# A two-stage network behind a decaying linear attention: early loads in a tile that is used later, a transfer rate in the planner's table, and a range check that is planned with the rest

## Chip, cores, metric

One core of a Trainium2 chip. The metric is the time of the program on the device in microseconds (us), the median of several runs; less is better. PE is TensorE, DVE VectorE, ACT ScalarE, POOL GpSimd, and SP SyncE, which here does nothing but issue DMAs.

## The reference

All is float32. An attention with a complex decay runs along the sequence (4 batches, 8 heads, 768 steps, 48 columns a head); its output is 3072 tokens of 384 numbers. A softplus layer pair follows, then a gated one. Cut to what matters:

```python
scale = np.minimum(mag, 0.999) / (mag + 1e-06)      # mag = |a_re + i a_im|
for t in range(S):
    S_re, S_im = ar * S_re - ai * S_im + kv, ar * S_im + ai * S_re   # kv = k_t v_t^T
    y[:, :, t] = q_t @ S_re
x = y as (3072, 384)
h = x @ w_in                                        # 384 -> 2048
x = (max(h, 0) + log1p(exp(-|h|))) @ w_out          # 2048 -> 384
h = (x @ w1) * (x @ w2) @ w3                        # 384 -> 1024 -> 1024
out = h @ w_out2                                    # 1024 -> 384
```

The weights of the layers come as 64-bit floats, which the kernel turns into 32-bit ones by integer operations on DVE.

## The kernel before

**Attention.** The sequence is cut into 24 chunks `u` of 128 steps; `u = 4 j + b` for step group `j` and batch `b`. For each chunk `load` brings the decay `a` (128 x 768), `load_qk` queries and keys `qk` (128 x 768), `load_v` the values. `norm` (steps s1 to s4) computes the magnitude and the limited decay: ACT squares `a` into `nt`, DVE adds, ACT takes logarithm and exponential, DVE multiplies the result with `a` into a tile `PT`, which holds two chunks. The multiply `PT<-a,nt` is the last reader of `a`. `scan` forms running products over two chunks on DVE (`tm`, `PT`, `ET`: first within groups of 8 steps, then over the group ends, then back down). `inv` forms the scaled queries and keys `qkp` from `PT` and `qk`, stores them to DRAM (`pd`) and reads them back in another layout (`rs`). `mm` makes the scores `sc` on PE, masks them on DVE (`am`), and multiplies with the values and the state (`yp`, `stp`) into `y`.

**Softplus stage.** 3072 tokens in blocks: 128, 128, 256 tokens (blocks 0 to 2), then five of 512 (blocks 3 to 7). For each of 16 slices `f` of the hidden layer, `s1` multiplies (`s`), ACT forms exp(-|h|) and its logarithm, DVE adds (`g`), and `s2a` accumulates in `acc`. Blocks 0 to 2 use plain float32 (`s<-x,w`). From block 3 on each factor is split into a high and a low half (`ww..h`, `ww..l`; `xh`, `xl`; both halves of `g` in the tile `gg`) and three products take the place of one (`s<-xh`); the low halves of the weights are formed on DVE during block 2. The attention's chunks for the next block run beside the block before. In the last block the weights of the gated stage are converted (`w3t`, `w12t`, `wo2t`), and w3 and w_out2 are multiplied into one matrix (`wpa`).

**Gated stage.** For six blocks of 512 tokens `s3` computes `pa` and `pb`, DVE multiplies them (`bg`), `s2b` accumulates with the combined matrix. Beside it all raw weights are loaded once more and their range is checked on DVE (`ck`, `lims`). At the end four comparisons (`okp`, line 1091), a reduce (`ok`, 1094), a transpose on PE (`okt`, 1098) and a reduce to one number (`oki`, 1099) decide whether a general version has to run.

**What sets the order.** Nothing is issued as it is written. Up to line 1078 the code records every instruction into a `Plan` (`add`), with what it depends on and a cost from a table (`cost`, from line 124). `flush` then runs a list scheduling 16 times with changing priorities, keeps the plan that ends earliest by the table, and issues the instructions in that order, from one helper line, 196. Each engine then runs its own queue strictly in that order; all DMAs stand in SP's queue, and one that has to wait holds up those behind it. In the table a DMA from DRAM to the chip takes SP `size / 360` ns, at least 475, and is there 2500 + `size / 360` ns after its start.

**Room.** A tile with a tag and `bufs=n` waits until the n-th last tile of that tag has had its last reader. `a` has one buffer (chunk 1 takes tag `n2` instead), `qk` has one (`QB = 1`), `v` one. The tile `gg` of tag `GG` (6 x 512 numbers in each partition) is first written in block 3:

```python
s["a"] = ap.tile([P, 2, GT], F32, tag="n2" if u == 1 else "a", bufs=1, name=f"a{u}")
s["qk"] = ap.tile([P, 2, GT], F32, tag="qk", bufs=QB, name=f"qk{u}")
gg.append(ap.tile([P, 2, HB, NB], F32R, tag="GG", name="gg"))
```

Of the kernel before, what the change touches and what calls it, by code (L numbers as in the profile page):

```python
# [11 lines left out]
F32 = mybir.dt.float32  # L12
F32R = mybir.dt.float32r
I32 = mybir.dt.int32
AF = mybir.ActivationFunctionType
ALU = mybir.AluOpType
PSUM = bass.MemoryType.PSUM
DRAM = bass.MemoryType.DRAM

P = 128  # L20
B, H, SEQ, D = 4, 8, 768, 48
DM = H * D
NT = B * SEQ
T = 128
NCH = NT // T
CPB = SEQ // T
G = DM // P
GT = G * T
# [3 lines left out]
NB = B * T  # L32
# [15 lines left out]
S1B = 5  # L48
ATAG = "s1"
VB = 1  # L50
TML = 384
NTB = 1
QB = 1
# [19 lines left out]
class Plan:  # L73
# [50 lines left out]
    def cost(self, eng, op, outs, ins):  # L124
        n = max(self.free_size(x) for x in (*outs, *ins))
        if eng == "SP":
            size = 4
            for _, n in outs[0].ap:
                size *= n
            cost = max(650 if n < 512 and self.on_chip(ins[0]) else 475, size / 360)  # L130
            if not self.on_chip(outs[0]):
                land = 5200
            elif self.on_chip(ins[0]):
                land = 2300
            elif hasattr(ins[0].tensor, "tag_meta"):
                land = 6800
            else:
                land = 2500 + size / 360
            return cost, max(land - cost, 0)
        if eng == "PE":  # L140
            n = self.free_size(outs[0])
            if op == "transpose":
                return 109, 250
            m = outs[0].ap[0][1]
            if ins[0].dtype == F32R:
                return n / 2.4 + 14, 250
            return (0.75 * n + 24 if m <= 64 else max(n, m) / 0.6 + 5), 250
        if eng == "DVE":
            far = [x for x in ins if x.ap[-1][0] >= 4 and x.ap[-1][1] > 1]
            return 72 + n / (1.92 if op == "tensor_scalar" else 0.52 if len(far) > 1 else 0.95), 200  # L150
        if eng == "ACT":
            return 105 + 0.88 * n, 200
        return 160 + n * 2.08, 200

    def push(self, eng, call, pre, cost, lat):
        self.ops.append((eng, call, pre, cost, lat))
        return len(self.ops) - 1

    def add(self, engine, op, args, kw):
# [35 lines left out]
        def call():  # L195
            getattr(engine.unit, op)(*args, **kw)  # L196

        cost, lat = self.cost(engine.name, op, outs, ins)
        if self.group is None:
            me = self.push(engine.name, [call], pre, cost, lat)  # L200
# [155 lines left out]
def fused(ctx: ExitStack, tc: tile.TileContext, a_in, qk_in, v_in, wio, w12, w3t, wo2, q, k, v, a_re, a_im, outT):  # L356
    nc = tc.nc
    plan = Plan(tc)
    V, A, PE, GP, SP = plan.V, plan.A, plan.PE, plan.GP, plan.SP

    fast = ExitStack()
# [5 lines left out]
    cp = ctx.enter_context(tc.tile_pool(name="cp", bufs=1))  # L367
# [3 lines left out]
    ap = fast.enter_context(tc.tile_pool(name="ap", bufs=1))  # L371
# [3 lines left out]
    ident = cp.tile([P, P], F32, name="ident")  # L375
# [8 lines left out]
        out=trow[:, 0:1], in0=trow[:, 2:3], scalar1=W - 1, scalar2=L.bit_length() - 1,  # L384
# [3 lines left out]
        out=trow[:, 1:2], in0=trow[:, 3:4], scalar1=W.bit_length() - 1, scalar2=None, op0=ALU.logical_shift_right  # L388
# [7 lines left out]
    m2max = cp.tile([P, NCH], F32, name="m2max")  # L396
    pend = cp.tile([P, B, G], F32, name="pend")
    NCK = 2 * FA + 6 * FB
    wlim = cp.tile([P, 2], F32, name="wlim")
    ncheck = [0]  # L400

# [14 lines left out]
    def pst(tag, bufs, shape, name):  # L416
        return ps.tile(shape, F32, tag=tag, bufs=bufs, name=name)

    def att_ps(shape, name):
        return pst(ATAG, ATT, shape, name)  # L420

    def load(u):
        s = c[u]
        s["a"] = ap.tile([P, 2, GT], F32, tag="n2" if u == 1 else "a", bufs=1, name=f"a{u}")
        SP.dma_start(s["a"], a_in[u])

    def load_qk(u):
        s = c[u]
        s["qk"] = ap.tile([P, 2, GT], F32, tag="qk", bufs=QB, name=f"qk{u}")
        SP.dma_start(s["qk"], qk_in[u])  # L430

    def load_v(u):
# [274 lines left out]
    def feed(u):  # L707
        load_qk(u)
        load_v(u)
# [3 lines left out]
    def norms(us):  # L713
        out = []
        for u in us:
            out += norm(u)
            if u + 1 < NCH:
                out.append(lambda u=u: load(u + 1))
        return out
# [165 lines left out]
    def evac_out(s):  # L885
        for i in range(KC):
# [7 lines left out]
            )  # L894

    load(0)
    for f in range(4):
        w_load(f)
# [82 lines left out]
    for bi in range(nblk):  # L981
        last = bi == nblk - 1
        t0, n = BLOCKS[bi]
# [29 lines left out]
    def b_x(bi):  # L1013
        r = ap.tile([P, 2 * H * T], F32, tag="rs1", name=f"xr{bi}")[:, 0 : KC * NB]
        r = r.rearrange("p (k n) -> p k n", k=KC)
        SP.dma_start(r, x2d[bi])
        if bi % 2:
            h, l = (ap.tile([P, KC, NB], F32R, tag="P", bufs=2, name=f"bx{n}{bi}") for n in "hl")
        else:
            h, l = x_tiles((f"bxh{bi}", f"bxl{bi}"))  # L1020
        split(h, l, r)
        xb[bi] = (h, l)
# [30 lines left out]
    for i, n in enumerate(("min", "max")):  # L1053
        bst[n] = lims[:, i * NCK : (i + 1) * NCK]
    b_x(0)
    it = 0
    nit = (NBB - 1) * FB
    for bi in range(NBB):
        gq = {}
        for f in range(FB):  # L1060
# [5 lines left out]
            it += 1  # L1066
            while ncheck[0] < min(NCK, NCK * it // nit):
                src, n = cks[ncheck[0]]
# [5 lines left out]
    for i, n in enumerate(("min", "max")):  # L1074
        V.tensor_reduce(
            out=wlim[:, i : i + 1], in_=bst[n], axis=mybir.AxisListType.X, op=getattr(ALU, n)
        )
    plan.flush()
    V, PE = nc.vector, nc.tensor
    fast.close()  # L1080
    ep = ctx.enter_context(tc.tile_pool(name="ep", bufs=1))
    okp = ep.tile([P, B * G + NCH + 2], F32, name="okp")
    c0 = 0
    for src, lim, op in (
        (pend.rearrange("p b g -> p (b g)"), 1e-3, ALU.is_ge),
# [4 lines left out]
        n = src.shape[1]  # L1090
        V.tensor_scalar(out=okp[:, c0 : c0 + n], in0=src, scalar1=lim, scalar2=None, op0=op)
        c0 += n
    ok1 = ep.tile([P, 1], F32, name="ok1")
    V.tensor_reduce(out=ok1, in_=okp, axis=mybir.AxisListType.X, op=ALU.min)
    oki = ep.tile([1, 1], I32, name="oki")
    with tc.tile_pool(name="fps", bufs=1, space=PSUM) as fps:
        okt = fps.tile([1, P], F32, name="okt")
        PE.transpose(okt, ok1, ident)
        V.tensor_reduce(out=oki, in_=okt, axis=mybir.AxisListType.X, op=ALU.min)
    ok = nc.values_load(oki[0:1, 0:1], min_val=0, max_val=1)  # L1100
    with tc.If(ok < 1):
        general(tc, q, k, v, a_re, a_im, wio, w12, w3t, wo2, xg, outT)
# [211 lines left out]
```

## Time and profile before

| what | value |
|---|---|
| median of 3 runs | 992.73 us (989.97 to 993.53) |
| profiled execution, own time | 990.76 us |
| its span | 989.0 us |
| mean granted clock of PE | 0.981 |
| PE matmul, busy | 883.0 us (89%), 5353 instructions |
| DVE, busy | 766.9 us (78%), 1713 instructions |
| ACT, busy | 520.5 us (53%), 1025 instructions |
| HBM read and written | 108.00 MB and 28.31 MB |

How to read it: the span is the time from the first to the last instruction of one execution; the profiled execution's own time has 1.8 us around it. Busy shares are averages over stages with different bounds, so the rows further down go stage by stage. All planned instructions bear line 196; a group is known by its tile. A timeline row gives start, duration, engine, line, operation, output and inputs, and in brackets the idle time just ahead of it with what ended it.

### The profile page before, as it was taken

What the parts mean: (1) busy time and instruction counts of PE and PEld (TensorE: products, weight loads), DVE (VectorE), ACT (ScalarE), POOL (GpSimd) and SP (SyncE); (2) the same over time, 40 slices, a digit from 0 to 9 for tenths busy, and PEclk for the clock granted to TensorE, in tenths of its full rate; (3) what the DMA queues carried; (4) which work ended last, traced back from release to release, by engine and by line L of the source; (5) the groups of instructions that cost most, each with busy time, mean ns of one, the idle gap of its engine ahead of it and who ended that gap; (6) DMA issues with size and microseconds to landing.
All of it is one profiled execution on the core that took longest, in us unless ns stands there. A gap on an engine that the chain in (4) does not pass through costs nothing.

```text
span 989.0 us, 15040 instructions
## 1 busy us (share of the span) xinstructions
PE 883.0 (89%) x5353; PEld 750.2 (76%) x5353; DVE 766.9 (78%) x1713; ACT 520.5 (53%) x1025; POOL 6.0 (1%) x19
## 2 busy tenths in 40 slices
PE   0048698886999999999999999999999999999996
PEld 0038597775888888888888888888888877788885
DVE  8998789889969998998997866977878787422221
ACT  4238677555867885778686664754231222131221
POOL 2000000000000000000000000000000000000000
PEclk9997899998999999999999999999999999999999
DMA  8490536473681656456375752444787867110101
GB/s 316 181 274 13 151 93 160 99 166 100 130 189 34 163 136 138 130 124 157 69 199 110 210 167 78 141 126 125 233 275 234 269 203 250 57 32 1 32 1 36
DMA packets 89938, 138.56 MB, mean 140 GB/s; under 512 B 7936, under 2 KB 60544, under 8 KB 89856
## 3 DMA queue, kind: packets, MB, share of 16 engines
q1 hardware_dynamic: 89856, 137.53, 50.4%
q8 instruction: 44, 0.72, 0.3%
q14 instruction: 38, 0.31, 0.1%
HBM read 108.00 MB, written 28.31 MB: 138 GB/s over the span
## 4 chain that ended last, share of the span: by engine, by line
PE 71%; DVE 15%; DMA 8%; issue 3%; ACT 3%; SPq 0%; POOL 0%; DVEq 0%; ACTq 0%; POOLq 0%
PE acc L196 26%; PE s L196 18%; PE pa L196 8%; PE pb L196 8%; DMA a<-a_in 4%; PE wpa L196 3%; DVE tm L196 3%; DVE PT L196 3%; PE sc L196 3%; PE yp L196 3%; DMA ckr<-w3t 2%; DVE w L196 2%; DVE qkp L196 1%; PE stp L196 1%; ACT nt L196 1%
## 5 line engine op out<-in xcount | busy, mean ns | idle before, releaser
L196 ACT ACTIVATE g<-g 128x512 f32<-128x512 f32 (+2 forms) x256 | 130.1, 521 | 3.3
L196 ACT ACTIVATE g<-s 128x512 f32<-128x512 f32 (+2 forms) x128 | 62.2, 487 | 68.2 <-PE s L196 45.1
L196 DVE TENSOR_TENSOR bg<-pa,bg 128x512 f32<-128x512 f32 x48 | 32.8, 687 | 80.9 <-PE pa L196 80.8
L196 DVE SCALAR_TENSOR_TENSOR g<-s,g 128x512 f32<-128x512 f32 (+2 forms) x128 | 70.8, 556 | 22.8 <-ACT g L196 22.4
L196 ACT CAST gg<-bg 128x512 fp32r<-128x512 f32 x48 | 29.8, 621 | 99.7 <-DVE bg L196 99.7
L196 ACT COPY bg<-pb 128x512 f32<-128x512 f32 x48 | 28.1, 587 | 90.5 <-PE pb L196 78.4
L196 PE MATMUL s<-x,w 128*128 128x128 f32 (+1 forms) x288 | 55.2, 340 | 16.5 <-DVE g L196 8.3
L196 PE MATMUL ktp<-ident,qkp 128*128 128x128 f32 x120 | 20.3, 290 | 54.7 <-DVE qkp L196 52.1
L196 PE MATMUL sc<-rs 112*128 112x128 f32 x384 | 53.3, 289 | 12.5 <-DMA rs<-pd 10.2
L196 PEld LDWEIGHTS sc<-rs 112*128 112x128 f32 x384 | 51.4, 203 | 16.4 <-issue 10.8
L196 DVE CUSTOM_DVE_ANT_0 ck<-ckr 128x384 f32<-128x384 f32 x80 | 43.5, 543 | 24.9 <-DMA ckr<-w3t 10.3
L196 PEld LDWEIGHTS s<-x,w 128*128 128x128 f32 x288 | 46.5, 215 | 20.8 <-DVE g L196 8.7
L196 ACT CAST gg<-g 128x512 fp32r<-128x512 f32 x80 | 49.2, 615 | 21.3 <-DVE g L196 12.7
L196 DVE TENSOR_TENSOR PT<-tm 128x96 f32<-128x96 f32 x192 | 59.3, 345 | 0.9
L196 PEld LDWEIGHTS ktp<-ident,qkp 128*128 128x128 f32 x120 | 15.3, 148 | 58.7 <-issue 47.3
L196 DVE TENSOR_TENSOR gg<-g,gg 128x512 fp32r<-128x512 f32 x80 | 55.1, 690 | 4.9 <-ACT gg L196 4.0
L196 PE MATMUL acc<-g,w 128*128 128x128 f32 (+1 forms) x288 | 51.5, 319 | 1.9 <-DVE g L196 1.9
L196 PE MATMUL acc<-gg,bwp2h 128*128 128x512 f32 x144 | 49.4, 392 | 1.2 <-ACT gg L196 1.2
L196 PE MATMUL acc<-gg,bwp0h 128*128 128x512 f32 x144 | 49.0, 392 | 1.1 <-ACT gg L196 1.1
L196 DVE TENSOR_TENSOR tm<-PT 128x384 f32<-128x384 f32 x84 | 46.9, 558 | 0.8
L196 PEld LDWEIGHTS acc<-g,w 128*128 128x128 f32 x288 | 42.9, 199 | 4.5 <-DVE g L196 2.3
L196 DVE TENSOR_REDUCE lims<-ck 128x1 f32<-128x384 f32 x80 | 43.1, 538 | 2.3
(314 smaller groups left out, 2313.0 us busy)
## 6 DMA issues: line engine op xcount, KB each, us to landing
pd<-qkp SPq DMA_DIRECT2D x24, 768.0 KB, 4.7
rs<-pd SPq DMA_DIRECT2D x48, 384.0 KB, 6.4
wr<-wio SPq DMA_DIRECT2D x32, 384.0 KB, 7.3
ckr<-wio SPq DMA_DIRECT2D x32, 384.0 KB, 3.7
a<-a_in SPq DMA_DIRECT2D x24, 384.0 KB, 3.4
qk<-qk_in SPq DMA_DIRECT2D x24, 384.0 KB, 3.8
w3r<-w3t SPq DMA_DIRECT2D x16, 384.0 KB, 3.6
w12r<-w SPq DMA_DIRECT2D x16, 384.0 KB, 3.2
```

Source lines behind the costliest of these rows:

```text
L196: getattr(engine.unit, op)(*args, **kw)
```

## The change

1. In the table, `size / 360` becomes `size / 270` in both places.
2. A tile `early` of tag `GG`, 4 x 768 numbers in each partition, takes `a2`, `a3`, `qk1` and `qk2`. They no longer use the tags `a` and `qk`.
3. The range check's last part is recorded ahead of `plan.flush()`, so that the plan orders it: `okp` takes a tile of tag `v`, `okt` one of tag `s1`, and `oki` lives in the pool `cp`, which stays open.

```diff
@@ cost
-            cost = max(650 if n < 512 and self.on_chip(ins[0]) else 475, size / 360)
+            cost = max(650 if n < 512 and self.on_chip(ins[0]) else 475, size / 270)
...
-                land = 2500 + size / 360
+                land = 2500 + size / 270
@@ fused
+    oki = cp.tile([1, 1], I32, name="oki")
...
+    ahead = []
+
+    def early():
+
+        if not ahead:
+            ahead.append(ap.tile([P, 4, 2, GT], F32, tag="GG", name="early"))
+        return ahead[0]
+
     def load(u):
         s = c[u]
-        s["a"] = ap.tile([P, 2, GT], F32, tag="n2" if u == 1 else "a", bufs=1, name=f"a{u}")
+        if u in (2, 3):
+            s["a"] = early()[:, u - 2]
+        else:
+            s["a"] = ap.tile([P, 2, GT], F32, tag="n2" if u == 1 else "a", bufs=1, name=f"a{u}")
         SP.dma_start(s["a"], a_in[u])
 
     def load_qk(u):
         s = c[u]
-        s["qk"] = ap.tile([P, 2, GT], F32, tag="qk", bufs=QB, name=f"qk{u}")
+        if u in (1, 2):
+            s["qk"] = early()[:, u + 1]
+        else:
+            s["qk"] = ap.tile([P, 2, GT], F32, tag="qk", bufs=QB, name=f"qk{u}")
         SP.dma_start(s["qk"], qk_in[u])
...
-    plan.flush()
-    V, PE = nc.vector, nc.tensor
-    fast.close()
-    ep = ctx.enter_context(tc.tile_pool(name="ep", bufs=1))
-    okp = ep.tile([P, B * G + NCH + 2], F32, name="okp")
+    okp = ap.tile([P, DM], F32, tag="v", bufs=VB, name="okp")
...
-    ok1 = ep.tile([P, 1], F32, name="ok1")
-    V.tensor_reduce(out=ok1, in_=okp, axis=mybir.AxisListType.X, op=ALU.min)
-    oki = ep.tile([1, 1], I32, name="oki")
-    with tc.tile_pool(name="fps", bufs=1, space=PSUM) as fps:
-        okt = fps.tile([1, P], F32, name="okt")
-        PE.transpose(okt, ok1, ident)
-        V.tensor_reduce(out=oki, in_=okt, axis=mybir.AxisListType.X, op=ALU.min)
+    ok1 = okp[:, DM - 1 : DM]
+    V.tensor_reduce(out=ok1, in_=okp[:, 0:c0], axis=mybir.AxisListType.X, op=ALU.min)
+    okt = pst("s1", S1B, [P, NB], "okt")[0:1, 0:P]
+    PE.transpose(okt, ok1, ident)
+    V.tensor_reduce(out=oki, in_=okt, axis=mybir.AxisListType.X, op=ALU.min)
+    plan.flush()
+    fast.close()
```

Since the order is planned as a whole, it changes on every engine. Three places are shown. A name ends in a number that differs between the programs; `y0` on SP is the moving of output rows between partitions, six small transfers, `x2d0` the store of a block's output.

SP's queue in block 1, the kernel before, around the load of chunk 3's queries and keys `qk3`:

```order
L196 DMA v1_164<-v_in 128x384
L196 DMA y0_161<-y0_161 16x128 x6
L196 DMA v2_282<-v_in 128x384
...
L196 DMA a5_328<-a_in 128x768
L196 DMA qk3_302<-qk_in 128x768
L196 DMA pd2_65<-qkp2_286 128x6x256
L196 DMA x2d0_57<-xoa0_0_240 128x128
L196 DMA x2d0_57<-xoa0_1_241 128x128
L196 DMA x2d0_57<-xoa0_2_242 128x128
L196 DMA qk4_355<-qk_in 128x768
L196 DMA rs0_129<-pd2_65 48x8x256 x2
L196 DMA pd3_66<-qkp3_307 128x6x256
```

and the changed one:

```order
L196 DMA v1_164<-v_in 128x384
L196 DMA qk3_300<-qk_in 128x768
L196 DMA v2_280<-v_in 128x384
L196 DMA y0_162<-y0_162 16x128 x6
L196 DMA a5_326<-a_in 128x768
L196 DMA x2d0_57<-xoa0_0_240 128x128
L196 DMA x2d0_57<-xoa0_1_241 128x128
L196 DMA x2d0_57<-xoa0_2_242 128x128
L196 DMA pd2_65<-qkp2_284 128x6x256
L196 DMA qk4_353<-qk_in 128x768
L196 DMA pd3_66<-qkp3_305 128x6x256
L196 DMA rs0_130<-pd2_65 48x8x256 x2
```

`qk3` has moved ahead of `v2` and of six small transfers; `pd2` has moved behind the three stores `x2d0`, and `pd3` ahead of the reading back of `pd2`.

DVE in block 2, the kernel before, up to the first step on the decay of chunk 9 (the ISA instruction on `nt9`) and the masks `am4` of chunk 4:

```order
L196 TENSOR_TENSOR ET1_122<-tm_408 128x6x12 x2
L196 TENSOR_TENSOR ww4l_486<-w32_4_188,ww4h_485 128x768
L196 TENSOR_TENSOR tm_409<-ET1_122 128x96
L196 TENSOR_TENSOR ww5l_493<-w32_5_195,ww4h_485 128x768
L196 TENSOR_TENSOR tm_409<-ET1_122 128x96
L196 SCALAR_TENSOR_TENSOR g_2_8_387<-s1_2_8_386,g_2_8_387 128x256
L196 TENSOR_TENSOR ET1_122<-tm_409 128x6x8 x2
L196 ISA nt9_457,m2max_118<-nt9_457 128x384
L196 ISA m2max_118 128x1
L196 TENSOR_TENSOR am4_0_364<-sc4_0_363,mask_109 128x512
L196 TENSOR_TENSOR tm_410<-PT3_389,ET1_122 128x768 x2
L196 TENSOR_TENSOR am4_1_366<-sc4_1_365,mask_109 128x512
```

and the changed one (`am4_1` stands three rows ahead of the first of these):

```order
L196 TENSOR_TENSOR ET1_123<-tm_407 128x6x8 x2
L196 TENSOR_TENSOR ww3l_474<-w32_3_184,ww2h_462 128x768
L196 TENSOR_TENSOR tm_408<-PT3_387,ET1_123 128x768 x2
L196 TENSOR_TENSOR am4_0_362<-sc4_0_361,mask_109 128x512
L196 TENSOR_TENSOR PT3_387<-tm_408 128x2x384
L196 SCALAR_TENSOR_TENSOR g_2_7_375<-s1_2_7_374,g_2_7_375 128x256
L196 TENSOR_TENSOR tm_409<-PT3_387,ET1_123 128x768 x2
L196 SCALAR_TENSOR_TENSOR g_2_8_385<-s1_2_8_384,g_2_8_385 128x256
L196 TENSOR_TENSOR PT3_387<-tm_409 128x2x384
L196 ISA nt9_455,m2max_118<-nt9_455 128x384
```

Both masks of chunk 4 and four products `tm` of 128x768 have moved ahead of `nt9`.

DVE at the end of block 2, the kernel before, around the last mask `am7_1` of the chunks that block 3 needs:

```order
L196 TENSOR_TENSOR ww11l_547<-w32_11_219,ww10h_538 128x768
...
L196 TENSOR_TENSOR am7_0_439<-sc7_0_438,mask_109 128x512
L196 SCALAR_TENSOR_TENSOR PT5_529<-PT5_529,nt11_531 128x8x48
L196 TENSOR_TENSOR tm_483<-PT4_455,ET0_121 128x768 x2
L196 TENSOR_TENSOR am7_1_441<-sc7_1_440,mask_109 128x512
```

and the changed one:

```order
L196 SCALAR_TENSOR_TENSOR PT5_527<-PT5_527,nt11_529 128x8x48
L196 TENSOR_TENSOR am7_1_439<-sc7_1_438,mask_109 128x512
L196 TENSOR_TENSOR tm_481<-PT4_453,ET0_122 128x768 x2
...
L196 TENSOR_TENSOR tm_482<-PT4_453,ET0_122 128x768 x2
L196 TENSOR_TENSOR S3_318<-stp7_441,S3_318 112x384
L196 TENSOR_TENSOR PT4_453<-tm_482 128x2x384
L196 TENSOR_TENSOR ww11l_545<-w32_11_219,ww10h_536 128x768
```

`ww11l` and two `tm` have moved from ahead of `am7_1` to behind it.

## Rows read from the trace of the kernel before

**Rows 1.** Windows: us; PE, PEld, DVE, ACT, POOL busy (count); PEclk, DMA share, GB/s

```profile
0.00:78.62 78.62, 12.80 (x92) 10.94 (x92) 74.26 (x150) 27.54 (x49) 6.03 (x19) 0.95 0.79 246
...
153.37:235.07 81.70, 66.41 (x536) 57.72 (x537) 74.27 (x180) 47.90 (x110) 0.00 (x0) 0.96 0.58 138
...
242.00:980.65 738.65, 735.21 (x4130) 616.27 (x4128) 550.10 (x1205) 387.46 (x701) 0.00 (x0) 1.00 0.49 135
...
50.00:75.00 25.00, 10.92 (x86) 9.73 (x86) 24.35 (x50) 7.99 (x14) 0.00 (x0) 0.92 1.07 273
...
119.87:125.80 5.93, 5.93 (x28) 5.93 (x29) 3.87 (x14) 1.70 (x7) 0.00 (x0) 0.50 1.01 255
...
589.13:652.42 63.29, 63.29 (x300) 54.83 (x299) 46.60 (x87) 42.14 (x73) 0.00 (x0) 1.00 0.32 93
```

**Rows 2.** Timeline of DVE, blocks 0 and 1: the instructions behind idle time

```profile
82.49 0.29 DVE L196 SCALAR_TENSOR_TENSOR g<-s,g 128x128 f32<-128x128 f32 x1 [2.54 <-ACT g L196]
...
109.32 0.56 DVE L196 TENSOR_TENSOR n<-n 128x384 f32<-128x384 f32 x1 [0.97 <-ACT n L196]
...
113.03 0.56 DVE L196 TENSOR_TENSOR qkp<-PT,qk 128x384 f32<-128x384 f32 x1 [3.15 <-DMA qk<-qk_in]
...
124.62 0.29 DVE L196 SCALAR_TENSOR_TENSOR g<-s,g 128x128 f32<-128x128 f32 x1 [1.96 <-ACT g L196]
```

**Rows 3.** Timeline of DVE, block 2

```profile
180.71 0.56 DVE L196 CUSTOM_DVE_ANT_0 nt<-nt 128x384 f32<-128x384 f32 x1 [4.00 <-ACT nt L196]
...
218.36 0.56 DVE L196 CUSTOM_DVE_ANT_0 nt<-nt 128x384 f32<-128x384 f32 x1 [2.71 <-ACT nt L196]
...
223.12 1.83 DVE L196 TENSOR_TENSOR tm<-PT,ET 128x768 f32<-128x768 f32 x2
224.86 0.69 DVE L196 TENSOR_TENSOR am<-sc,mask 128x512 f32<-128x512 f32 x1
```

**Rows 4.** Chain that ended last: start, duration, what (from issue to use)

```profile
107.24 5.76 DMA qk<-qk_in
...
172.07 7.68 DMA a<-a_in
...
210.31 7.09 DMA a<-a_in
```

**Rows 5.** Timeline of SP's queue: issues, with the time they took there

```profile
100.63 0.33 SPq L196 DMA_DIRECT2D v<-v_in  x1
...
107.24 0.33 SPq L196 DMA_DIRECT2D qk<-qk_in  x1
...
109.47 2.82 SPq L196 DMA_DIRECT2D x2d<-xoa  x3
...
171.15 0.83 SPq L196 DMA_DIRECT2D rs<-pd  x2
172.07 0.42 SPq L196 DMA_DIRECT2D a<-a_in  x1
```

**Rows 6.** Timeline of PE

```profile
119.87 1.65 PE L196 MATMUL s<-x,w 128*128 128x128 f32 x6 [8.13 <-DVE g L196]
...
176.16 1.06 PE L196 MATMUL sc<-rs 112*128 112x128 f32 x8
...
235.07 1.22 PE L196 MATMUL s<-xh,ww0h 128*128 128x512 f32 x2 [7.69 <-ACT xh L196]
...
980.26 0.39 PE L196 MATMUL acc<-gg,bwp2h 128*128 128x512 f32 x1
```

**Rows 7.** Timeline of DVE at the end

```profile
980.68 0.17 DVE L1091 TENSOR_SCALAR okp<-pend 128x12 f32<-128x12 f32 x1 [3.30 <-PE acc L196]
...
981.73 0.28 DVE L1099 TENSOR_REDUCE oki<-okt 1x1 int32<-1x128 f32 x1 [0.45 <-PE okt L1098]
```

**Rows 8.** The decay loads `a`, all 24 issues

```profile
DMA to landing us min/median/max: 2.9/3.4/9.5
```

**Rows 9.** Groups of DVE from 500 to 660 us: busy, mean ns of one, idle ahead

```profile
L196 DVE SCALAR_TENSOR_TENSOR w3t<-w3r,w3t 128x384 int32<-128x384 int32 x30 | 16.7, 555 | 0.4
```

## Prediction

> **What bounds the kernel now.** I read the windows first, then the gaps on VectorE (DVE), then SyncE's queue (SP) at each gap, and last the end of the program.
>
> The windows [rows 1] are cut at 235.07 us, where the first split product starts, the matmul into `s` from `xh` [rows 6]. Behind it TensorE (PE) is the bound: from 242.00 to 980.65 it is busy 735.21 of 738.65 us at a granted clock of 1.00, DVE 550.10. Ahead of it DVE is the bound: 74.26 of the first 78.62 us, and 74.27 of the 81.70 that end at 235.07, where PE has 66.41. In the printed order 624 matmuls of PE stand ahead of that product in both programs, so the work left behind it is the same. The argument is short, then: what moves 235.07 moves the end one for one, plus what happens behind the last matmul.
>
> The idle pieces of DVE ahead of 235.07 can be named. Four stand in blocks 0 and 1 [rows 2]: 2.54 us for a softplus sum, 0.97 for the inverse `n`, 3.15 for the queries and keys of chunk 3, 1.96 for another softplus sum. Two stand in block 2 [rows 3]: 4.00 us at `nt9` and 2.71 at `nt11`. These two are charged to ScalarE, whose square had itself waited for a decay load: in the chain of waits [rows 4] the loads `qk3`, `a9` and `a11` took 5.76, 7.68 and 7.09 us from issue to use.
>
> **The change, part by part.** The sum is made against the profiled execution, 990.76 us (span 989.0).
>
> *Early loads, start.* `a2`, `a3`, `qk1` and `qk2` no longer wait for a slot of the tags `a` and `qk`. At most this returns the idle time of the first window, 78.62 − 74.26 = 4.4 us, at least nothing, since these loads share the DMA engines with the weights: from 50 to 75 us the engines are booked at 1.07 of their time [rows 1]. DVE has the same work there; I take 0.7, nearer to nothing.
>
> *Early loads, block 1.* The clearest term. With one `qk` slot, `qk3` cannot be issued before `qk2` has its last reader; SP issues it at 107.24 [rows 5], and DVE stands 3.15 us for it at 113.03 [rows 2]. In the new order `qk3` is ahead of `v2`, which was issued at 100.63 [rows 5]. Even with 5.76 us on the way it then lands near 106.4, over 6 us ahead of its use. Saved 3.1 us (bounds: 0 if `v1` ahead of it is held back, 4.1 if the 0.97 goes too). Next to be late there is DVE's own work.
>
> *PE's gap.* The same stall leaves PE idle for 8.13 us [rows 6], and behind it PE is granted 0.50 of its clock, 1.2 in place of 2.4 GHz: from 119.87 to 125.80 it has 28 matmul records in 5.93 us [rows 1], 2.97 at the full level. A part is on the path, since DVE stands 1.96 us for the softplus sum behind these products [rows 2]. With the gap cut to a few us I count 2.0 saved (0 if the clock drops all the same, 2.97 if all was on the path).
>
> *The table, 270 in place of 360.* A load of 384 KB is planned to land 0.36 us later (393,216/270 − 393,216/360 ns). That is small, but it reorders DVE. The work between the multiply that frees `a` for `a9` and `nt9` was small pieces, three low halves `ww` and three sums, 5.9 us with each instruction at its traced duration, against 7.68 for the load and 0.85 for its square; hence the 4.00. In the new order both mask multiplies `am4` and four more `tm` of 128x768 (0.87 each: 223.12 to 224.86 for two [rows 3]) stand there, 10.7 us in all, and the 4.00 goes. It has a price: the scores that `am4` reads began on PE at 176.16 [rows 6]. In the new order one or two first-layer tiles fewer stand ahead of them, but DVE asks for `am4_1` behind 152.0 us of work where it was 160.1. I count 2.0 us of new waiting (bounds 0 and 3.5). At `nt11` the cover shrinks from 7.9 to 6.4 us, so its wait grows by 1.5. Net −0.5 (−4.0 to +1.0).
>
> *What block 3 needs.* Its input is the output of chunks 4 to 7, so the last mask multiply that it needs is `am7_1`. In the old order a low half `ww11l` and two `tm` of 128x768 stand ahead of it (the two `tm` just ahead, 224.86 behind 223.12 [rows 3]); in the new order all three stand behind it: 3 × 0.87 = 2.6 us off the path (0 if PE's scores then come late).
>
> *SP's queue.* `pd2` now stands behind the three stores of block 0's output, which took SP from 109.47 to 112.29 [rows 5], and `pd3` ahead of the reading back of `pd2`. `pd2` may be 3 to 4 us later, its reading back 1 to 2. PE reads that for the scores of chunk 2 well behind 119.87, where first-layer tiles come first; cost 0, up to 2 if this cover is gone.
>
> *The end.* The last accumulation starts at 980.26 [rows 6], and the check that follows takes to 982.01 [rows 7]. The comparisons and the first reduce move into the gated stage, about 1 us where DVE has room; PE's transpose and the last reduce stay. Saved 0.8 (0 to 1.3).
>
> **A rule against it.** A load of `a` lands in 2.9 us at best, 3.4 in the median, 9.5 at worst [rows 8]. A lone load thus fits the old rate better, 2.5 + 1.09 = 3.6 us, than the new, 2.5 + 1.46 = 4.0. What stalls DVE is the tail: `a9` was issued at 172.07, right behind two reads back at 171.15 [rows 5], which no rate in the table expresses. Of a full queue the rows show 273 GB/s between 50 and 75 us [rows 1].
>
> The Trainium skill, "DMA: Bandwidth & Descriptors", section "Where 436 GB/s comes from", puts the limit of HBM for one core near 358 GB/s, so that 270 would be a false correction; the trace agrees for a lone load and not for the full queue. By that rule the sum would lack its two terms of order and be −6.6 in place of −9.7.
>
> I keep both terms, since they come from the printed order.
>
> **Sum.** −0.7 − 3.1 − 2.0 − 0.5 − 2.6 − 0.8 = −9.7. The first three feed one chain through block 1, and an idle piece that goes is partly found again at the next wait, so I take −8.7: 982.1 in the profiled execution. The median of the runs, 992.73, lies 1.97 above the profiled execution; the forecast is **984.0 us**.
>
> **Rivals.**
>
> 1. *Given back before 235.07.* The waits move: `am4` at its full 3.5 us, `nt11` at more than 1.5, chunk 2's scores at 2. For it: an earlier DVE asks earlier for loads that leave behind the same reads back. Against it: the stall on `qk3` has a cause, and that is removed. The 9.7 then shrink by 1.5 + 2 + about 2 to some 4: 992.7 − 4 = 989. Chance 0.18.
>
> 2. *More.* The upper ends: 2.5 at the start (the 2.54 of [rows 2]), 4.1, 2.97, 2.5 at `nt9` and `nt11` with `am4` waiting for nothing, 2.6 and 1.3 are 16; with the overlap 14 or 15: 978. Chance 0.12.
>
> 3. *The rate was right, the new order is a mere draw.* As a mechanism of this kernel: 0.36 us says nothing of a wait of 4.00, the planner only lands elsewhere, and the terms −0.5 and −2.6 fall out: 9.7 − 3.1 = 6.6 are left, 992.7 − 6.6 = 986. Chance 0.15. This is what the page's rule would make of it.
>
> 4. *Slower: weight conversion in block 7.* From 589.13 to 652.42, between the first and last softplus sum of block 7, PE is busy all the time and DVE 46.60 us [rows 1]. From the one to the other the old order has 83 instructions of DVE, the new 124: conversions that come earlier, 0.555 us for the commonest kind [rows 9], 41 × 0.555 = 23 us at most. If PE's matmuls of the conversion did not come along, DVE's 46.6 + 23 = 70 would outrun PE's 63.3, and late `gg` halves would hold PE in its order. It decides from 17 us added. The excess is 7 us; with each late half also starting PE's next tile late, I price it at twice that, 14: 984 + 14 = 998. Against it: part of PE's conversion matmuls stand there too. Chance 0.07.
>
> 5. *Nothing.* New waits eat all of it: 992. Chance 0.06.
>
> The forecast itself, 981 to 987, keeps 0.42.
>
> **How the numbers follow.** Half a per cent, 5 us, is about what a measurement of this kernel can tell from no change. Faster by more (below 987.8): the forecast 0.42, rival 2 0.12, rival 3 0.13, and 0.04 of rival 1, together 0.71. Same: 0.14 of rival 1, 0.02 of rival 3, 0.06 of rival 5, 0.01 of rival 4, together 0.23. Slower: 0.06. The range runs from 975, rival 2's lower end, to 991, which takes in rival 1; rivals 4 and 5 and the far ends lie outside.
>
> **What would show it.** Right: the first product from `xh` starts near 227 us; DVE waits for no `qk`; no stretch of clock 0.50 near 120 us; no idle of 4 us at `nt9`; one transpose and one reduce behind the last accumulation. Wrong: that product at 232 or later (rival 1); a gap of 3 us at `am4`; PE idle for 10 us and more in block 7 (rival 4). If that product moves and the end does not follow it, then "one for one" is the false step.

## The result, and the profile after

The change makes the kernel faster: 976.55 us median of 4 runs (975.64 to 977.33) against 991.55 in the same comparison, a ratio of 0.9847, 95% interval 0.9824 to 0.9871. That lies in the range, near its lower end; the gain is 15 us, about twice the 7.5 to 8.7 us that were forecast. The profiled execution took 976.20 us, its span is 974.4.

The windows of the changed kernel, cut where those of [rows 1] are cut (us; PE, PEld, DVE, ACT and POOL busy with counts; granted PE clock, DMA share, GB/s):

```profile
0.00:77.80 77.80, 12.72 (x93) 11.43 (x93) 72.62 (x146) 29.19 (x50) 6.04 (x19) 1.00 0.77 250
147.74:222.86 75.12, 66.40 (x537) 58.27 (x537) 72.13 (x177) 47.25 (x108) 0.00 (x0) 0.93 0.61 150
222.86:229.79 6.93, 6.93 (x21) 5.48 (x21) 6.93 (x19) 1.91 (x4) 0.00 (x0) 0.65 0.08 17
229.79:966.28 736.49, 735.00 (x4134) 617.36 (x4132) 555.25 (x1219) 386.91 (x702) 0.00 (x0) 1.00 0.49 137
575.24:652.43 77.19, 77.19 (x371) 67.52 (x371) 65.07 (x130) 46.85 (x84) 0.00 (x0) 1.00 0.45 134
112.81:117.50 4.69, 4.69 (x22) 4.69 (x23) 3.17 (x9) 2.22 (x7) 0.00 (x0) 0.50 1.08 291
```

Of the 14.6 us that the span lost, 12.2 lie ahead of the first split product, which now starts at 222.86. From there to the end of the last accumulation it is 743.4 us where it was 745.6, and behind that 8.1 instead of 8.3. In block 7 DVE has much of the load that rival 4 named, 65.07 us busy in 77.19, and PE is busy all the time.

DVE at the places of [rows 2, 3]: the step behind `qk3`, `nt9`, the masks `am4` and `nt11`, from its timeline:

```profile
107.99 0.56 DVE L196 TENSOR_TENSOR n<-n 128x384 f32<-128x384 f32 x1 [0.97 <-ACT n L196]
...
168.39 0.69 DVE L196 TENSOR_TENSOR am<-sc,mask 128x512 f32<-128x512 f32 x1 [0.24 <-PE sc L196]
...
177.61 0.55 DVE L196 CUSTOM_DVE_ANT_0 nt<-nt 128x384 f32<-128x384 f32 x1
...
207.47 0.56 DVE L196 CUSTOM_DVE_ANT_0 nt<-nt 128x384 f32<-128x384 f32 x1 [0.97 <-ACT nt L196]
```

No wait on `qk` is left, none at `nt9`, 0.24 us at `am4`, and 0.97 at `nt11` where 2.71 stood. PE, at the places of [rows 6]:

```profile
112.81 1.65 PE L196 MATMUL s<-x,w 128*128 128x128 f32 x6 [4.10 <-DVE g L196]
...
116.81 1.49 PE L196 MATMUL acc<-g,w 128*128 128x128 f32 x6
118.09 1.02 PE L196 MATMUL s<-x,w 128*128 128x128 f32 x6
...
222.86 1.22 PE L196 MATMUL s<-xh,ww0h 128*128 128x512 f32 x2 [7.35 <-ACT xh L196]
```

The gap near 115 us is 4.10 instead of 8.13, and the clock still drops behind it: the last window above has 22 matmul records at 0.50, and six matmuls take 1.49 us up to 118 us.

The decay loads that go to the tile `a`, 22 of the 24, and below them the four loads of the tile `early` (`a2`, `a3`, `qk1`, `qk2`):

```profile
DMA to landing us min/median/max: 2.8/3.4/7.3
```

```profile
DMA to landing us min/median/max: 5.8/7.7/8.3
```

A lone load lands as fast as in [rows 8]. The slowest took 9.5 there and at most 8.3 here.

Block 2, cut in both kernels from its first softplus sum to the first split product, before and after:

```profile
159.19:235.07 75.88, 60.59 (x518) 52.84 (x517) 68.52 (x164) 44.66 (x103) 0.00 (x0) 0.98 0.56 129
```

```profile
153.74:222.86 69.12, 60.40 (x522) 53.39 (x520) 67.35 (x163) 44.89 (x103) 0.00 (x0) 0.96 0.59 141
```

This stretch is 6.8 us shorter: DVE is idle for 1.8 us in place of 7.4, and has 1.2 us less work in it.

### The profile page after: what moved, and what is told of

Read it like the earlier page. It is cut to its first block, busy times and chain, and to the rows that moved or that the text cites. A ratio compares the mean times of both kernels' runs of the same rounds, so it can differ in the third digit from the quotient of the medians.

```text
span 974.4 us, 15024 instructions
## 1 busy us (share of the span) xinstructions
PE 881.1 (90%) x5353; PEld 750.7 (77%) x5353; DVE 769.5 (79%) x1713; ACT 520.3 (53%) x1025; POOL 6.0 (1%) x19
## 4 chain that ended last, share of the span: by engine, by line
PE 58%; DMA 3%; DVE 2%; issue 1%; ACT 0%; SPq 0%; DVEq 0%
PE acc L196 21%; PE s L196 12%; PE pa L196 8%; PE pb L196 8%; PE wpa L196 3%; PE yp L196 2%; PE sc L196 2%; DMA ckr<-w 2%; DMA ckr<-w3t 1%; PE stp L196 1%; DVE ck L196 1%; DVE lims L196 1%; PE ktp L196 0%; DVE bg L196 0%; DVE gg L196 0%
## 5 line engine op out<-in xcount | busy, mean ns | idle before, releaser
L196 PEld LDWEIGHTS sc<-rs 112*128 112x128 f32 x384 | 48.9, 198 | 7.3 <-issue 4.3
L196 PE MATMUL sc<-rs 112*128 112x128 f32 x384 | 50.3, 283 | 4.5 <-DMA rs<-pd 3.9
L196 DVE TENSOR_TENSOR gg<-bg,gg 128x512 fp32r<-128x512 f32 x48 | 33.0, 688 | 16.2 <-ACT gg L196 16.2
```

## The experiments

Theory A is that of the prediction: each part pays for the stall that it removes. Theory B: the planner's search lands on some order, the old one was a poor one, and any new one gains. Theory C, formed after the first eight runs: the rate in the table does it.

**One part at a time.** The two lines of the rate; the early tile; the ordered check; the tile and the rate.

```diff
@@ e1_table and e4_early_table
-            cost = max(650 if n < 512 and self.on_chip(ins[0]) else 475, size / 360)
+            cost = max(650 if n < 512 and self.on_chip(ins[0]) else 475, size / 270)
-                land = 2500 + size / 360
+                land = 2500 + size / 270
@@ e2_early and e4_early_table (load, and load_qk likewise, as in the change)
+        if u in (2, 3):
+            s["a"] = early()[:, u - 2]
@@ e3_check (as in the change)
-    plan.flush()
...
+    okp = ap.tile([P, DM], F32, tag="v", bufs=VB, name="okp")
...
+    plan.flush()
```

> The kernel before with the rate 270 alone. Theory A (each part pays for its own stall): queries and keys of chunk 3 still wait for the one qk slot, so the 3.15 us stall and the half-clock stretch near 120 us stay; between the multiply that frees a for a9 and nt9 the planned DVE work is 6.1 us by traced durations (5.4 before), so that wait stays above 2 us; gain 0 to 4 us, 987 to 992. Theory B (the plan is a draw, any new order gains because the old one was a poor one ahead of block 3): DVE work ahead of am7_1 falls from 199.8 to 190.9 us, and the first split product moves by as much as in the changed kernel, 8 us or more; 979 to 984.

> The kernel before with the early tile alone, rate 360. Theory A: the qk stall and the half-clock stretch go (qk3 is issued ahead of chunk 0's store), cover ahead of nt9 7.2 us, so about 2 us of wait are left there; gain 6 to 9 us, 983 to 986. Theory B: any new order gains, 978 to 984, with no relation to which waits the part removes. If the early tile is worth nothing without the table: 989 to 993.

> The kernel before with the range check ordered by the plan, rate 360, no early tile. Theory A: the end behind the last accumulation is set by the last output copy and its store, not by the check, so it stays about 8.1 to 8.3 us; ahead of block 3 the qk stall stays; 989 to 992. Theory B: the recorded instructions at the end change the priorities of the whole plan, so the order ahead of block 3 is another draw: 980 to 986.

> The change without the ordered check. Theory A: the gain of the change less at most 0.8 us for the end: 976 to 979. Theory B: another order, a gain anywhere from 5 to 15 us.

The rate alone took 964.27 us (ratio 0.9745, 0.9725 to 0.9766), the early tile alone 982.24 (0.9938, 0.9914 to 0.9963), the check alone 977.83 (0.989, 0.9859 to 0.992), tile and rate 969.40 (0.9807, 0.9775 to 0.9839). Theory A falls: the parts' gains add up to far more than the whole, and the smallest piece of the diff alone beats the whole change by 12 us (10 by the ratios, since the kernel before took 991.55 us in the comparison of the whole change and 989.25 in this one). Theory B did not foresee the sizes either: only the early tile came out where it was expected; the rate alone, the check alone and tile with rate are faster than any range above. With the rate alone `qk` has one slot as before, and yet no DVE wait on it is left. SP's timeline of that kernel has `qk3` as the first row below, nearly 4 us earlier than the 107.24 of [rows 5]; its first split product finds PE hardly idle and keeps the full clock, 1.00 (PE's timeline, then the window behind it):

```profile
103.43 0.33 SPq L196 DMA_DIRECT2D qk<-qk_in  x1
```

```profile
214.26 1.19 PE L196 MATMUL s<-xh,ww0h 128*128 128x512 f32 x4 [1.75 <-ACT xh L196]
```

```profile
214.26:221.19 6.93, 6.92 (x30) 5.74 (x31) 6.93 (x11) 2.92 (x8) 0.00 (x0) 1.00 0.13 42
```

**Another draw of the same plan.** Only the seed of the noise in the planner's second round, in the kernel before and in the changed one.

```diff
@@ s1_before and s1_after (2 in s2_before and s2_after)
-SEED = 214
+SEED = 1
```

> The kernel before with another number for the noise in the planner's second round (SEED 1 in place of 214) and nothing else. Theory B (the time is that of the order that the search happens to land on; the order of the kernel before is a poor one): 965 to 983, the first split product between 213 and 224 us, with the qk3 stall absent though the early tile, the rate and the ordered check are all absent. Theory A (the parts pay): 986 to 993, with the stalls on qk3 and nt9 still there.

> The same with SEED 2. Theory B: 965 to 983; two seeds differ from each other by some us. Theory A: 986 to 993.

> The changed kernel with SEED 1. Theory B: 965 to 983, and not lower than the kernel before with other seeds by more than these scatter. Theory A: the parts are worth 10 us and more at every seed, so some 10 us below the kernel before at the same seed.

> The changed kernel with SEED 2. Theory B: 965 to 983, no more than a few us from the kernel before at the same seed, either way. Theory A: some 10 us below it.

The kernel before took 995.81 us with one seed (ratio 1.0062, 1.0034 to 1.009) and 977.76 with the other (0.9888, 0.9854 to 0.9923); the changed kernel 974.80 (0.9842) and 969.52 (0.9799). So a seed alone moves the kernel before by 18 us, more than the change does. With SEED 1 its wait on `qk` is 0.3 us, at the old rate and with one slot, and yet it took 995.81 us, outside both ranges: its first split product starts 9.0 us earlier than in the kernel before, and its span, 994.8 us, is 5.8 longer. With SEED 2 the changed kernel is 8 us below the kernel before, nearer theory A's 10 than theory B's few. But the five plans at 270 were all below the five at 360 (the nearest two by 1.2 us, 976.55 and 977.76), which pure chance does not favour. That gave theory C.

**The rate alone at other seeds, and half of it.**

```diff
@@ r_cost_only, this line alone
-            cost = max(650 if n < 512 and self.on_chip(ins[0]) else 475, size / 360)
+            cost = max(650 if n < 512 and self.on_chip(ins[0]) else 475, size / 270)
@@ r_land_only, this line alone
-                land = 2500 + size / 360
+                land = 2500 + size / 270
```

> The rate 270 alone (no early tile, no ordered check), SEED 1. Theory C (the rate does it: five plans at 270 took 964 to 977 us, five at 360 took 978 to 996, with 0.6 to 2.5 us of idle TensorE behind the first split product against 3.4 to 11.9): 964 to 977, some 20 us below the kernel before at this seed (995.8), idle TensorE behind the split product below 3 us. Theory B (pure draw over all plans): 964 to 996 with nothing to say which.

> The rate 270 alone, SEED 2. Theory C: 964 to 977, below the kernel before at this seed (977.8). Theory B: 964 to 996. If the early tile adds a gain of its own, this and the other two seeds without it (one took 964.3) lie above the changed kernel at the same seeds (976.6, 974.8, 969.5).

> The kernel before with 270 only in the time that a transfer holds the queue of SyncE, 360 in its landing. If the gain of the rate comes from spacing the transfers, 964 to 977 with idle TensorE below 3 us behind the split product; if it comes from the later landing of each load, 978 to 990.

> The kernel before with 270 only in the landing of a load, 360 in the time that it holds the queue. If the gain of the rate comes from the later landing (0.36 us a load of 384 KB), 964 to 977; if from the spacing, 978 to 990.

968.56 us (0.9795, 0.9773 to 0.9817) and 969.80 (0.9804, 0.978 to 0.9827): as theory C has it. Either half alone gave 973.67 (0.9849) and 973.43 (0.9844). Each lies in the range that its expectation gave to its own half, above the three plans with the whole rate alone and below all plans at 360. It is one plan each, so the question of spacing or landing stays undecided, and that each does a part is not shown.

**More slack, and the early tile at the old rate.** 200 in both places; the early tile alone with the other two seeds.

```diff
@@ r200 (both places)
-                land = 2500 + size / 360
+                land = 2500 + size / 200
@@ s1_early (2 in s2_early): e2_early with
-SEED = 214
+SEED = 1
```

> The kernel before with the rate at 200 in both places. If more slack for loads in the plan always helps, below 968 and nearly no wait at nt; if 270 is near the best, 965 to 980 with other work pushed later (work ahead of the mask am7_1 is 199.8 us again by traced durations, 190.9 at 270).

> The early tile alone at rate 360, SEED 1. If the early tile is worth 7 us by itself, as at SEED 214 (982.2 against 989): 985 to 991, below the kernel before at this seed (995.8). If its plans are draws from the same scatter as any at 360: 977 to 996.

> The early tile alone at rate 360, SEED 2. If it is worth 7 us and more by itself, as at the other two seeds, 962 to 971, below the kernel before at this seed (977.8). If the plans at 360 are one scatter with and without it: 977 to 985.

At 200 it is 980.36 us (0.9893, 0.9861 to 0.9926): more slack was not better in this one plan. The early tile at 360 took 978.89 (0.9884) and 986.25 (0.9978); the second is above both of its ranges, and only the scatter of plans is left as an account of the two. Medians by seed, in us:

| seed | neither part, 360 | early tile, 360 | rate 270 alone | whole change |
|---|---|---|---|---|
| 214 | 989.25 | 982.24 | 964.27 | 976.55 |
| 1 | 995.81 | 978.89 | 968.56 | 974.80 |
| 2 | 977.76 | 986.25 | 969.80 | 969.52 |

The rate gains 25, 27 and 8 us without the other parts. The early tile at the old rate gains 7 and 17 and loses 8; tile and check on top of the rate lose 12 (10 by the ratios) and 6 and gain 0.3.

Cut at the first split product and at the end of the last accumulation, the profiled executions show where the rate acts (us; idle PE is that behind the product):

| kernels | first split product | from there to the last accumulation | idle PE |
|---|---|---|---|
| before, s1_before, s2_before | 235.1, 226.0, 220.4 | 745.6, 760.1, 746.2 | 3.4, 11.9, 3.8 |
| e2_early, s1_early, s2_early | 218.4, 220.2, 227.2 | 753.0, 748.4, 746.8 | 8.7, 4.5, 3.9 |
| e3_check | 219.3 | 749.3 | 7.2 |
| r_cost_only, r_land_only | 219.9, 218.3 | 744.0, 745.0 | 2.5, 4.3 |
| e1_table, s1_table, s2_table | 214.3, 217.4, 219.4 | 741.0, 742.2, 740.8 | 2.5, 0.9, 0.3 |
| e4_early_table | 218.9 | 740.2 | 1.5 |
| after, s1_after, s2_after | 222.9, 224.1, 218.2 | 743.4, 742.3, 742.1 | 1.5, 2.4, 0.6 |
| r200 | 229.7 | 741.0 | 1.0 |

Behind the product the groups do not touch: 745.6 to 760.1 at 360, 744.0 and 745.0 with half of the rate, 740.2 to 743.4 at 270. Each figure is one execution; another one of the old plan, in which only a mask ahead of the product was moved (h4_am7_first, below), took 749.6 where the kernel before took 745.6. Ahead of it the groups overlap; there the kernel before has the latest start of all, and r200 the next. What PE waits for behind the product, at 360 in the worst plan (s1_before) and at 270 in e1_table (waits of PE: what waited, for what, us in all, times, the longest):

```profile
PE stp L196 <- DVE g L196: 4.8, 3, 2.8
PE s L196 <- ACT xh L196: 4.0, 1, 4.0
PE acc L196 <- ACT gg L196: 2.6, 3, 1.4
```

```profile
PE s L196 <- ACT xh L196: 1.8, 1, 1.8
PE s L196 <- DVE g L196: 1.1, 1, 1.1
```

In both PE stands for tiles of DVE and ACT that come late, at 360 for longer. These engines wait for DMAs in their turn. The two longest of ACT's waits for DMAs in the same stretch, again s1_before and then e1_table (`outT<-o` is the store of a result):

```profile
ACT bg L196 <- DMA outT<-o: 12.6, 4, 6.3
ACT nt L196 <- DMA a<-a_in: 11.3, 6, 3.0
```

```profile
ACT bg L196 <- DMA outT<-o: 7.6, 3, 3.0
ACT nt L196 <- DMA a<-a_in: 1.7, 1, 1.7
```

ACT's waits for all DMAs there sum to 19.3 to 26.7 us in the seven plans at 360, 10.8 and 11.9 with half of the rate, 6.6 to 14.6 in the seven at 270, and 4.4 at 200. So with more allowance in the table ACT waits less for DMAs behind the product. That this is what shortens PE's waits was not tried by moving such a wait alone.

**The old plan held, one thing moved.** These three keep the plan and move one row or a few in one queue; the other queues keep their order.

```diff
@@ flush of the changed kernel, behind the plan: h2_qk3_back
+        k = find("SP", "dma_start", "qk3")
+        line.remove(k)
+        line.insert(line.index(find("SP", "dma_start", "a5")) + 1, k)
@@ flush of the kernel before: h3_five_later (needs: the row or its queue depends on k)
+        for name, us in (("nt9", 4.0), ("nt11", 2.7), ("nt13", 3.2), ("nt19", 3.4), ("nt23", 1.5)):
+            k = find("DVE", "tensor_tensor_reduce", name)
+            i, t = line.index(k), 0
+            line.remove(k)
+            while t < 1000 * us and not needs(line[i], k):
+                t += self.ops[line[i]][3]
+                i += 1
+            line.insert(i, k)
@@ flush of the kernel before: h4_am7_first (ww11l then goes behind am7_1)
+        k = find("DVE", "tensor_tensor", "am7_1")
+        line.remove(k)
+        line.insert(line.index(find("DVE", "tensor_tensor", "am7_0")) + 1, k)
```

> The changed kernel with its plan held on every engine and one edit: qk3 goes back behind a5 in the queue of SyncE, where the kernel before had it. If the term of 3.1 us for the qk stall is right, a wait of some us on qk3 comes back and the first split product moves from 222.9 to 225 to 227 us, the time to about 979 to 981. If the early tile and the order already gave qk3 room, nothing: 975 to 978.

> The plan of the kernel before, held on every engine, with five first steps nt9, nt11, nt13, nt19 and nt23 moved later in VectorE's queue (by three to eight instructions where the data allow it). If the waits for decay loads cost what they show, the first split product comes 4 to 6 us earlier (235 to about 230) and the end 4 to 8: 982 to 986. If such idle pieces are found again at the next wait: the product moves by less than 2 us and the time stays at 987 to 991.

> The plan of the kernel before, held on every engine, with the mask am7_1 moved ahead of the two products tm and of ww11l in VectorE's queue. If the term of the prediction is right (2.6 us of work off the path), the first split product comes about 2.6 us earlier and the time is 986 to 988. Rival: by the timeline of ScalarE in the kernel before, the copy of chunk 7's output waits 4.00 us behind a copy into ET that needs VectorE's scan of the next pair, not the mask; then nothing moves, 987 to 991.

`qk3` put back: 978.23 us (0.9874, 0.984 to 0.9909), and in DVE's timeline the wait is there again. The first split product moves from 222.86 to 225.57, and the span grows by 1.9 us. Of the 2.7 us at the product 0.6 were there ahead of the wait already (the softplus sum at 99.74 stands at 100.39 in this execution), so about 2.1 come with the wait. The time lies between the two expected ranges:

```profile
108.17 0.56 DVE L197 TENSOR_TENSOR qkp<-PT,qk 128x384 f32<-128x384 f32 x1 [3.36 <-DMA qk<-qk_in]
```

Five steps later: 994.29 us (1.0054, 1.0036 to 1.0072), slightly slower, not faster; the product starts at 234.74, although this execution was 2.9 us ahead at the first softplus sum of block 2, before any moved row; from that sum to the product it took 78.5 us in place of 75.9. The 4.00 at `nt9` is gone from DVE and found again. By the chain of waits of this kernel the load of `a9` takes 7.42 us, then ACT squares it, and only then, in its own queue, makes the copy into `ET` that DVE's products wait for:

```profile
168.96 7.42 DMA a<-a_in
176.42 0.04 issue
176.46 0.84 ACT nt L197
177.31 0.18 ACT ET L197
177.51 0.96 DVE tm L197
```

The load holds ACT's queue too, so moving DVE's part of it bought nothing here.

The mask first: 990.29 us (1.0007, 0.9991 to 1.0023), nothing. The rival of its expectation holds. ACT's timeline of this kernel shows the copy of the output `y` still standing behind the copy into `ET`, which waits for DVE's `tm`:

```profile
227.45 0.21 ACT L197 COPY ET<-PT 128x12 f32<-128x12 f32 x1 [3.53 <-DVE tm L197]
227.57 1.18 ACT L197 COPY y<-yp 48x512 f32<-48x512 f32 x2
```

The product starts 1.3 us earlier in that execution, but that execution was 2.1 us ahead already at the first softplus sum of block 2, long before the moved row.

## Why the prediction was right in sign and wrong in size

Right: what moves the first split product moves the end, 12.2 of 14.6 us here. But "one for one" rests on "the work left behind it is the same", and that is no full answer: the same matmuls took 740 to 760 us behind it in different plans, and with SEED 1 the old kernel starts the product 9.0 us earlier and ends 5.8 later. I put nothing on that part, and it gave 2.2.

Right in sign: the term on `qk3`, 3.1 us. The wait is gone, and putting that one load back brings 3.36 of it back, of which about 2.1 reach the product. But 3.1 was the size of one execution; up to this wait the held plan of h3_five_later is that of the kernel before, and there it is

```profile
110.25 0.56 DVE L197 TENSOR_TENSOR qkp<-PT,qk 128x384 f32<-128x384 f32 x1 [1.79 <-DMA qk<-qk_in]
```

and 1.82 in h4_am7_first. Its cause was wrong, too: neither the early tile nor the rate is needed for it, since with one slot the wait is gone in e1_table, is 0.3 with SEED 1 at 360, and is gone in e3_check at 360.

Right by luck, in part: start, `qk3` and the half-clock stretch together were −5.8, and the first softplus sum of block 2 is 5.5 us earlier (159.19 to 153.74). The start alone was 0.7 (measured 0.8). But the clock's 2.0 did not come as I had it, as the stretch at 0.50 is still there behind a gap of 4.10. Instead DVE's waits at 82.49 and 88.37 shrank, 2.54 and 1.33 to 0.49 and nothing. My list of idle pieces lacked that 1.33 and two more of 1.06 (118.06) and 0.99 (127.37), and I had read no window from 78.62 to 153.37, where DVE was busy for only 60.83 of 74.75 us: there it is not the bound by itself.

Wrong: block 2, the step "net −0.5" with the 2.6 for `am7_1`, −3.1 together. From that sum to the split product it took 75.9 us and now 69.1: −6.8. By the two windows of block 2 above, DVE's idle time fell by 5.6 us, where the step had 0.5; the work moved off the path is 1.2, where I had 2.6. The new waits that I charged did not come, 0.24 us at `am4` instead of 2.0, and `nt11` lost 1.7 instead of gaining 1.5. That is 5.0 of difference, more than the missing 3.7.

The mechanism of the two gains is not shown either: in the held plan, moving `nt9` and four steps like it gave nothing because ACT's queue carries the same wait, and moving the mask gave nothing because the copy that follows it stands behind another one in ACT's queue. In the changed plan the wait for `a9` has left both queues, and at `a11` ACT waits for DVE instead of the load. ACT's row for `a9`, before and after:

```profile
179.83 0.84 ACT L196 ACTIVATE nt<-a 128x768 f32<-128x768 f32 x1 [3.91 <-DMA a<-a_in]
```

```profile
173.49 0.83 ACT L196 ACTIVATE nt<-a 128x768 f32<-128x768 f32 x1
```

So DVE and ACT would have had to be read together here. No run moves both, so which rows of the new order gave the 5.6 stays open.

Wrong: the end, −0.8, gave −0.2. Every plan has 8.0 to 8.7 us behind the last accumulation, whether the check is ordered or not, so the check doesn't set most of it; what does, the last output store or the branch behind the check, was not tried.

Wrong in weight: rival 3, "the rate was right, the new order is a mere draw", at 0.15. Half of it is so: a seed moves the kernel before by 18 us, and the start of the split product is largely such a draw (the old plan's 235.1 is the latest of 17 planned kernels). The other half is the reverse of it: the rate is what helped at all three seeds. The Trainium skill, "DMA: Bandwidth & Descriptors", section "Where 436 GB/s comes from", has about 358 GB/s as the limit of HBM for one core. A lone load of `a` does not speak against the old rate: its best landing is 2.9 us before and 2.8 after, below the 3.6 that the old rate plans. But the 273 GB/s of [rows 1] that I set against it is not the rate of every full queue. In the kernel before, the DMA engines moved 410 GB/s early in the program, more than those 358, booked at 1.03:

```profile
10.00:15.00 5.00, 0.00 (x0) 0.00 (x0) 4.95 (x9) 2.15 (x5) 0.00 (x0) 1.00 1.03 410
```

As a rate for the planner 360 is nevertheless the worse number here. The likely reason, argued and not tested by itself, is that loads behind others land after 5.8 to 9.5 us ([rows 4, 8]) and in-order queues wait for them.

Rival 4 did not come: the 47 to 65 us of DVE in block 7 fit, since the matmuls of the conversion moved along (371 records instead of 300).

Left open: which of ACT's shorter waits for DMAs give the 270 plans their shorter second part; whether spacing or landing matters more; whether the early tile is worth anything at 360, where its three plans lie inside the scatter. The best kernel measured is the rate alone at the old seed, 964.27 us, 12 us below the whole change; with a scatter of some 6 us among plans at 270, part of that is luck too.

## What to carry to other kernels

Where a planner orders a whole program, first run the unchanged kernel with other seeds: here that scatter, 18 us, is larger than the change, and no edit can be judged on one plan a side. A wait in an in-order queue is worth what it shows only if no other queue carries the same wait, so move the one row in the held plan before crediting it; and read it in more than one execution, since the same row waited 3.15, 1.79 and 1.82 us here. A transfer rate in such a table worked here as an allowance for crowded queues rather than as the speed of a lone transfer: with 270 in place of 360 the time fell at all three seeds, and the one plan with 200 was slower than every plan with 270.

## What was not expected of the hardware

PE's clock fell to 0.50 behind an idle gap of 4.10 us as it had behind 8.13; with half the gap the slow stretch, 5.7 us (26 matmul records from 112.81 to 118.50, all at 0.50), was about as long as the 5.93 of [rows 1]. Behind the gap of 7.35 us ahead of the split product the window at 222.86 shows 0.65, and behind e1_table's 1.75 us it shows 1.00.
